# LSH attention and two MLPs: a quarter of the first batch's P transposed by TensorE instead of the DMA, and the low parts of q and V moved to GpSimd there

## The chip, the cores and the metric

One core of one Trainium2 chip runs the whole program. The metric is the device time of one execution in microseconds; lower is better. The kernel before takes 832.61 us, the median of 3 runs (831.09 to 833.43).

## The reference

The inputs are q, k and v of 2 batches, 8 heads, 768 positions and 64 dimensions, a projection of 64 x 6, and the weights of two MLPs (512 to 2048 and back), in float64.

```python
bits   = (q @ proj > 0), (k @ proj > 0)          # 6 bits: a bucket for each position
scores = q @ k.T / sqrt(64), -1e9 where the buckets of q and k differ
attn   = softmax(scores); x = attn @ v           # heads side by side: 1536 x 512
x = gelu_like(x @ w_in) @ w_out                  # h * sigmoid(1.702 h)
x = silu(x @ w_in2) @ w_out2                     # h * sigmoid(h)
```

## The kernel before

Every value is carried as two parts, a rounded high part and a low part that holds the rest, so that several cheap matmuls stand for one exact product. The float64 weights are taken apart on the chip (lines 167 to 178).

The program has three stages. **Stage 0** is attention on the first batch alone, **stage 1** is attention on the second batch with the first MLP on the first batch's tokens running in between (`mlp`, drawn by credits of `RATE`), and **stage 2** is what is left of both MLPs. `stage[0]` turns from 0 to 1 at step 51 of the loop in `attention`, when the 48 steps of the first batch have been written out.

Attention goes in **steps**: step `j` is 128 queries of one head against all 768 keys. There are 96, 48 in each batch; steps 2m and 2m + 1 make a **pair of steps**, 24 in each batch. One step does this:

- `scores` (line 404, 405): TensorE writes the scores, with the mask added by a second matmul, to PSUM.
- `top` (line 422): VectorE takes them from PSUM to `p` and finds the row's extreme.
- `exps` (line 427): ScalarE takes the exponential in place. `p` is 128 x 768 in float32, and there are three buffers of it in stage 0.
- `p_high` (lines 436, 438): `p` is cast to float16, by VectorE for steps with `j % 5` of 2 or 4 (`HIGHV`), else by ScalarE, into the pair's tile `hl` (three buffers in stage 0).
- `p_low` (line 442): GpSimd subtracts the high part from `p`, which gives the low part in float16.
- `p_turn` (line 448): after the second step of a pair, one DMA transposes the whole `hl` tile, 128 x 3072 in float16 (786 KB), into `pt`, of which there are two buffers (`PTB`). SyncE issues it. It comes one step later than the step's other work (`TUL`).
- `av` (lines 460 to 462): TensorE multiplies the 12 blocks of `pt` that belong to the step with V's two parts, 18 matmuls. It is written out three steps after the step's exponential (`LAG`).
- `norm`, `x_turn`, `x_split` (lines 472 to 495): after a head's six steps the rows are scaled, transposed by TensorE into PSUM and split into `XH` (ScalarE) and `XL` (VectorE), as the MLPs read them.

Each head needs preparation, which `ahead` spreads over the 12 steps of the pair of heads before it. `natural` (lines 292, 293) splits q and k into parts: the high part by VectorE, the low part by the engine that `LOWG` names for the stage (GpSimd for k in stage 0 and for k, q in stage 1, if the head is not one of the first two). `turn` (line 300) transposes them on TensorE through a PSUM tile of the pool `ps_m`, which has two buffers, `evict` (line 307) takes them out by ScalarE, `move` copies half of them by ScalarE or a DMA, `bits` and `signs` (lines 332, 339) make the buckets, and `rows` (line 347) moves these by DMA. V is scaled and split by `v_max`, `v_spread`, `v_scale`, `v_high` (line 383, ScalarE) and `v_low`: one VectorE instruction (line 392) in stage 0, a ScalarE scaling in place and a GpSimd subtraction (lines 389, 390) in stage 1.

All transfers but two small ones are issued by SyncE, in one order: the loads of q, k and v, the moves, the rows, the weights and the transposes stand in one queue. Each engine works through its instructions in a fixed order. That order comes from the build: a scheduler arranges the instructions by priority, and `sooner` puts a task of a kind ahead by the number in `SOONER` (for `p_high` 200 in stage 0, `p_low` 75, `p_turn` 35, `natural` 800).

Of the kernel before, what the change touches and what calls it, by code (L numbers as in the profile page):

```python
# [9 lines left out]
F32 = mybir.dt.float32  # L10
F32R = mybir.dt.float32r
F16 = mybir.dt.float16
# [3 lines left out]
ALU = mybir.AluOpType  # L16
# [5 lines left out]
def tile_lsh_attention_two_mlps(  # L22
# [13 lines left out]
    V, A, G, T, SP = nc.vector, nc.scalar, nc.gpsimd, nc.tensor, nc.sync  # L36
# [5 lines left out]
    P = 128  # L42
    NC = S // P
    HS = S // 2
    HC = NC // 2
# [20 lines left out]
    PTB = 2  # L66
    EARLY = 0
    WSTART = 38
    WEVERY = 3
    LOWG = ('k', 'kqv')  # L70
    COPY = ('k', 'q')
    FB = 2
    PB = 2
# [1 line left out]
    GB = 2  # L75

    HIGHV = ((5, (2, 4)), (1, ()))


    SOONER = ({'ahead': 100, 'move': 20, 'load_v': 400, 'evict': 200, 'p_high': 200, 'natural': 800, 'p_turn': 35, 'turn': 100, 'p_low': 75, 'top': 35, 'exps': 75, 'bits': 300, 'norm': 35, 'load': 50, 'signs': 20}, {'scores': 200, 'evict': 50, 'norm': 300, 'av': 400, 'natural': 200, 'gate': 50, 'p_turn': 20, 'load_v': 200, 'load': 20, 'sum': 150, 'move': 20, 'p_high': 150, 'rows': 100, 'p_low': 75, 'bits': 100, 'exps': 20}, {'gate': 300, 'sum': 10, 'weights': 50})  # L80
# [5 lines left out]
    stage = [0]  # L86
# [162 lines left out]
    def attention(sp, s1, ps_m, ps_v, ahead_of, setup):  # L249
        nat, st = {}, {}  # L250
# [12 lines left out]
        N = len(steps)  # L263
# [9 lines left out]
        VS, ident, identr, vtop, pa, pb, thr, thrq, BQ, BK = setup()  # L273
# [13 lines left out]
        def natural(n, nm):  # L287
            x = nat[n, nm]
            hp, lp = (1, 0) if nm == "q" else (0, 1)
            E = G if nm in LOWG[stage[0]] and n > 1 else V  # L290
            t = sp.tile([P, NC, 2, D], F32R, tag="s" + nm, name="s" + nm, bufs=1)
# [93 lines left out]
        def v_low(pr, j):  # L385
            vs, s = st["v", pr]
            x = nat[pr, "v"][:, j]
            if "v" in LOWG[stage[0]]:
                A.activation(x, x, AF.Copy, scale=s[:, j:j + 1])
# [21 lines left out]
        def rotate(tag, bufs, shape, dtype):  # L411
            pool, more = ahead_of["more"].get(tag, (None, 0))
            j = count[tag] = (count.get(tag, -1) + 1) % (bufs + more)
            if j < bufs:
                return sp.tile(shape, dtype, tag=tag, name=tag, bufs=bufs)
            return pool.tile(shape, dtype, tag=tag, name=tag, bufs=more)
# [10 lines left out]
            A.activation(p, p, AF.Exp, bias=lo, scale=-1.0)  # L427


        def p_high(j):  # L430
            if j % 2 == 0:
                st["hl", j] = st["hl", j + 1] = rotate("hl", HLB, [P, 2, 2, 2, HS], F16)
            hl, p = st["hl", j][:, j % 2, 0], st["p", j][0]
            m, own = HIGHV[stage[0]]
            if j % m in own:
                V.tensor_copy(hl, p)
            else:
                A.copy(hl, p)  # L438

        def p_low(j):  # L440
            hl = st["hl", j][:, j % 2]
            G.tensor_tensor(out=hl[:, 1], in0=st.pop(("p", j))[0], in1=hl[:, 0], op=ALU.subtract)  # L442

        def p_turn(j):
            hl = st.pop(("hl", j))
            if j % 2 == 1:
                pt = rotate("pt", PTB, [P, 4 * NC, P], F16)
                latest[0] = SP.dma_start_transpose(out=pt, in_=hl.rearrange("p s a b c -> p (s a b c)")).ins
                st["pt", j - 1], st["pt", j] = pt[:, 0:2 * NC], pt[:, 2 * NC:]
# [109 lines left out]
        for lead, first, last in ((2, 0, N // 2), (1, N // 2, N)):  # L559
            def at(f, j):  # L560
                if first <= j < last:
                    with sooner(f.__name__):
                        f(j)

            for i in range(first - lead, last + LAG + 1):
                if lead == 2:
                    at(scores, i + 2)
                at(av, i - LAG)
                at(top, i + lead - 1)
                m = i - LAG  # L570
                if first <= m < last and m == group[m][-1]:
                    with sooner("norm"):
                        norm(group[m])
                m = i - 2 * (2 - lead)
                if first <= m < last:
                    pr, s = divmod(m, 2 * NC)
                    with sooner("ahead"):
                        if pr + 1 < HEADS // 2:
                            run(ahead(pr + 1, s))
                        if s >= 2 * NC - 4 and pr + 2 < HEADS // 2:  # L580
                            run(ahead(pr + 2, s - 2 * NC))
                at(exps, i)
                at(p_high, i)
                at(p_low, i)
                at(p_turn, i - TUL)
                yield i
                if lead == 1:
                    at(scores, i + 1)
# [107 lines left out]
    with ExitStack() as es:  # L696
        ps_m = es.enter_context(tc.tile_pool(name="ps_m", bufs=2, space=PSUM))
# [8 lines left out]
        for i in attention(sp, s1, ps_m, ps_v, ahead_of, lambda: attention_setup(sp, s1, am, ps_m)):  # L706
            if i == -2:
                for _ in range(EARLY):
                    W.fetch()
            if gen is None and i >= WSTART and i % WEVERY == 0 and W.done < 4:  # L710
                W.step()
            if gen is None and i == SWITCH - 1:
                ps_s.close()
                stage[0] = 1
                ahead_of["lead"] = 1
                ahead_of["more"] = {}
                mb = es.enter_context(tc.tile_pool(name="mlpb", bufs=2))
                ahead_of["pool"] = es.enter_context(tc.tile_pool(name="ps_s1", bufs=1, space=PSUM))
                ps_h = es.enter_context(tc.tile_pool(name="ps_h", bufs=2, space=PSUM))
                gen = mlp(0, [0, 1], [[f, f + 1] for f in range(0, NF, 2)], W, mb, ps_h, True, first1)  # L720
            if gen is not None:
                credit += RATE[i >= 3 * HEADS // 4 * NC]
                while credit >= 1.0:
                    credit -= 1.0
                    next(gen, None)
                    background()
# [41 lines left out]
```

## Time and profile before

| what | us |
|---|---|
| median of 3 runs | 832.61 |
| the profiled execution | 831.93 |
| its span, from the first to the last instruction | 830.1 |

| stage | from, to (us) | length (us) |
|---|---|---|
| 0, attention of the first batch, after the first loads | 20 to 165 | 145 |
| 1, attention of the second batch beside the first MLP | 165 to 415 | 250 |
| 2, the rest of the MLPs | 415 to 830.1 | 415.1 |

The profile is one execution. Busy time of an engine is the union of its instructions' spans; PE is TensorE's matmuls, PEld its weight loads, DVE VectorE, ACT ScalarE, POOL GpSimd, SP SyncE, of which only the queue (SPq) matters here. PEclk is the granted clock of TensorE as a share of full speed. The DMA share is the mean busy share of 16 DMA engines by the time that their packets took. The borders of the stages are read from the work that runs: the first batch's last transpose is issued at 162.6 us, and the last of all at 408.2 us.

### The profile page before, as it was taken

Reading aid. Unit: us, or ns where it says so; the run is one execution under the profiler, and the core shown is the slowest. Engines: PE = TensorE matmul, PEld = TensorE weight load, DVE = VectorE, ACT = ScalarE, POOL = GpSimd, SP = SyncE. Lnnn points to the kernel's source line nnn. Section 1 sums busy time; section 2 is a strip of 40 time slices with the busy share of each in tenths; the row PEclk is TensorE's granted clock in tenths of the full one; section 3 lists DMA queues with packets and bytes.
Section 4 is the critical chain, followed back from the end, with each engine's and each line's share of the span. In section 5 each row is a group of like instructions: output and inputs, shape, how many; then the busy total and the mean of one; then the engine's idle time right before and its main releaser. Section 6 shows DMA issues by size and latency. Waiting matters only on the chain.

```text
span 830.1 us, 13998 instructions
## 1 busy us (share of the span) xinstructions
PE 753.3 (91%) x5384; PEld 692.9 (83%) x5384; DVE 533.9 (64%) x932; ACT 421.4 (51%) x721; POOL 442.0 (53%) x345
## 2 busy tenths in 40 slices
PE   6787787698898998988999999979999999999998
PEld 5677576577797887887999999979999989998996
DVE  8877787988689889779424233899733843422222
ACT  6758656596675666655534232444645433321220
POOL 5656676777777857766733242549534533421120
PEclk9778979599999999999999999999999999999999
DMA  4999999998998979865587421232310400000112
GB/s 117 190 180 193 200 180 223 231 247 238 246 254 231 223 216 226 210 153 109 108 300 261 150 104 49 77 127 95 108 51 21 132 2 1 0 1 1 39 39 76
DMA packets 196270, 116.40 MB, mean 140 GB/s; under 512 B 153318, under 2 KB 175846, under 8 KB 196204
## 3 DMA queue, kind: packets, MB, share of 16 engines
q1 hardware_dynamic: 196044, 115.52, 55.8%
q8 instruction: 42, 0.69, 0.3%
q14 instruction: 24, 0.20, 0.1%
q10 hardware_dynamic: 160, 0.00, 0.0%
HBM read 56.63 MB, written 16.78 MB: 88 GB/s over the span
## 4 chain that ended last, share of the span: by engine, by line
PE 59%; DVE 20%; DMA 10%; ACT 5%; issue 4%; POOL 1%; SPq 1%; DVEq 0%; ACTq 0%; POOLq 0%
PE pso L642 26%; PE psh L608 25%; DMA pt<-hl 6%; DVE f L173 3%; DVE p L422 3%; DVE f L171 3%; DVE f L175 2%; DVE f L172 2%; PE pss L404 2%; PE pss L405 1%; PE psbit L332 1%; POOL hl L442 1%; DMA nk<-in_k_dram 1%; PE pav L460 1%; ACT p L427 1%
## 5 line engine op out<-in xcount | busy, mean ns | idle before, releaser
L619 POOL TENSOR_TENSOR gl<-g,gh 128x384 fp32r<-128x384 f32 x128 | 138.3, 1081 | 201.7 <-ACT gh L618 189.5
L442 POOL TENSOR_TENSOR hl<-p,hl 128x768 f16<-128x768 f32 x96 | 168.0, 1757 | 75.7 <-ACT hl L438 33.2
L608 PE MATMUL psh<-XH,wih 128*128 128x384 f32 x512 | 174.2, 340 | 6.0 <-DVE part L651 3.9
L608 PE MATMUL psh<-XH,wil 128*128 128x384 f32 x512 | 173.0, 338 | 0.0
L608 PE MATMUL psh<-XL,wih 128*128 128x384 f32 x512 | 172.9, 338 | 0.0
L617 DVE TENSOR_TENSOR g<-g,psh 128x384 f32<-128x384 f32 x96 | 52.7, 550 | 116.8 <-ACT g L616 116.7
L651 DVE SCALAR_TENSOR_TENSOR part<-pso,part 128x384 f32<-128x384 f32 (+1 forms) x124 | 72.6, 590 | 83.0 <-PE pso L642 82.8
L427 ACT ACTIVATE p<-p,lo 128x768 f32<-128x768 f32 x96 | 89.7, 937 | 70.4 <-DVE p L422 70.2
L618 ACT CAST gh<-g 128x384 fp32r<-128x384 f32 x128 | 65.5, 512 | 86.7 <-DVE g L617 70.7
L608 PEld LDWEIGHTS psh<-XH,wih 128*128 128x128 f32 x512 | 97.2, 190 | 8.1 <-DVE g L614 2.2
L642 PE MATMUL pso<-gh,woh 128*128 128x384 f32 x256 | 88.6, 352 | 16.9 <-DVE g L614 7.0
L422 DVE TENSOR_SCALAR_CACHE_REDUCE p<-pss 128x768 f32<-128x768 f32 x96 | 90.8, 947 | 14.9 <-PE pss L405 8.6
L608 PEld LDWEIGHTS psh<-XL,wih 128*128 128x128 f32 x512 | 97.2, 190 | 0.6
L608 PEld LDWEIGHTS psh<-XH,wil 128*128 128x128 f32 x512 | 97.2, 190 | 0.0
L616 ACT ACTIVATE g<-psh 128x384 f32<-128x384 f32 x96 | 46.8, 488 | 96.2 <-PE psh L608 95.2
L404 PE MATMUL pss<-ak,aq 128*128 128x384 f32 x192 | 77.4, 404 | 19.7 <-DVE p L422 19.5
L642 PE MATMUL pso<-gl,woh 128*128 128x384 f32 x256 | 86.5, 338 | 0.0
L642 PE MATMUL pso<-gh,wol 128*128 128x384 f32 x256 | 86.5, 338 | 0.0
L460 PE MATMUL pav<-VS,pt 128*128 128x65 f16 x576 | 69.4, 205 | 15.4 <-DMA pt<-hl 13.0
L460 PEld LDWEIGHTS <-pt 128*128 128x128 f16 x576 | 57.4, 105 | 24.1 <-DMA pt<-hl 17.7
L642 PE MATMUL pso<-woh,gh 128*128 128x512 f32 x192 | 74.9, 390 | 0.2 <-ACT gh L618 0.2
L642 PE MATMUL pso<-wol,gh 128*128 128x512 f32 x192 | 75.0, 391 | 0.0
(114 smaller groups left out, 1623.1 us busy)
## 6 DMA issues: line engine op xcount, KB each, us to landing
raw<-in_moe_w_in_dram SPq DMA_DIRECT2D x32, 512.0 KB
raw<-in_moe_w_out_dram SPq DMA_DIRECT2D x32, 512.0 KB
spih<-wih SPq DMA_DIRECT2D x13, 256.0 KB
spil<-wil SPq DMA_DIRECT2D x13, 256.0 KB
spoh<-woh SPq DMA_DIRECT2D x13, 256.0 KB
spol<-wol SPq DMA_DIRECT2D x13, 256.0 KB
wih<-spih SPq DMA_DIRECT2D x13, 256.0 KB
wil<-spil SPq DMA_DIRECT2D x13, 256.0 KB
```

Source lines behind the costliest of these rows:

```text
L404: T.matmul(o, lhsT=lq, rhs=ak[:, half, :], start=True, stop=False)
L422: V.tensor_scalar(p, st.pop(("S", j)), LOW, None, op0=ALU.min, op1=ALU.min, accum_out=lo)
L427: A.activation(p, p, AF.Exp, bias=lo, scale=-1.0)
L442: G.tensor_tensor(out=hl[:, 1], in0=st.pop(("p", j))[0], in1=hl[:, 0], op=ALU.subtract)
L460: T.matmul(o, lhsT=pt[:, i], rhs=hv, start=(i == 0), stop=False)
L608: T.matmul(h, lhsT=a[:, c], rhs=x[t][:, c], start=(n == 0), stop=(n == 3 * NDC - 1))
L616: A.activation(g, h, AF.Sigmoid, scale=beta)
L617: V.tensor_tensor(out=g, in0=g, in1=h, op=ALU.mult)
L618: A.copy(gh[:, f], g)
L619: G.tensor_tensor(out=gl[:, f], in0=g, in1=gh[:, f].bitcast(F32), op=ALU.subtract)
L642: T.matmul(y, lhsT=a, rhs=x, start=(n == 0), stop=(n == 3 * nf - 1))
L651: V.scalar_tensor_tensor(out=acc, in0=y, scalar=scale, in1=acc, op0=ALU.mult, op1=ALU.add)
```

## The change

In stage 0 the pairs of steps 3, 7, 11, 15, 19 and 23 (`TURNT`: of every four pairs the last) are not cast and transposed as before. `p_parts` takes the place of `p_high`, `p_low` and `p_turn` for them. TensorE transposes `p` itself in float32, 128 x 128 at a time, three blocks to a PSUM tile of `ps_m`; ScalarE casts the tile's 128 x 384 to float16 straight into `pt`, and VectorE subtracts that from the PSUM tile and writes the low part into `pt`. A step takes two such tiles. The pair's `pt` buffer is taken when its first step is at `p_high`, not at `p_turn`. Besides, `LOWG` of stage 0 becomes that of stage 1: q's low part (heads after the first two) goes to GpSimd, and V's low part to ScalarE and GpSimd. Nothing in stages 1 and 2 is changed.

```diff
-    LOWG = ('k', 'kqv')
+    LOWG = ('kqv', 'kqv')
+    TURNT = ((4, (3,)), (1, ()))
...
+        def by_tensor(j):
+            m, own = TURNT[stage[0]] if j < N // 2 else TURNT[1]
+            return j // 2 % m in own
+
+        def p_parts(j):
+            if j % 2 == 0:
+                st["whole", j] = st["whole", j + 1] = rotate("pt", PTB, [P, 4 * NC, P], F16)
+            p = st.pop(("p", j))[0]
+            pt = st.pop(("whole", j))[:, j % 2 * 2 * NC:(j % 2 + 1) * 2 * NC]
+            for a in range(2):
+                ps = ps_m.tile([P, 512], F32, tag="m", name="psp")
+                for i in range(HC):
+                    T.transpose(ps[:, i * P:(i + 1) * P], p[:, a, i * P:(i + 1) * P], ident)
+                x = ps[:, 0:HS].rearrange("p (c q) -> p c q", c=HC)
+                hi, lo = (pt[:, n + a * HC:n + (a + 1) * HC] for n in (0, NC))
+                A.copy(hi, x)
+                V.tensor_tensor(out=lo, in0=x, in1=hi, op=ALU.subtract)
+            st["pt", j] = pt
+
         def p_high(j):
+            if by_tensor(j):
+                return p_parts(j)
...
         def p_low(j):
+            if by_tensor(j):
+                return
...
         def p_turn(j):
+            if by_tensor(j):
+                return
```

## Rows read from the trace of the kernel before

**Rows 1.** Busy time of each engine in stretches of the run (us from the span's start): the stretch, its length, busy us and number of instructions of PE, PEld, DVE, ACT and POOL, the granted clock of TensorE, the DMA share and the GB/s moved.

```profile
20.00:165.00 145.00, 111.35 (x1186) 96.76 (x1187) 118.86 (x216) 96.33 (x140) 96.17 (x61) 0.80 1.00 198
50.00:140.00 90.00, 71.90 (x841) 60.86 (x840) 72.60 (x140) 63.76 (x93) 60.52 (x38) 0.89 1.01 192
165.00:415.00 250.00, 222.90 (x1980) 204.38 (x1979) 203.80 (x358) 164.23 (x271) 174.43 (x125) 0.97 0.86 205
415.00:830.10 415.10, 406.00 (x2147) 381.52 (x2145) 193.88 (x301) 148.71 (x291) 160.69 (x142) 1.00 0.24 82
```

**Rows 2.** The same view for two shorter stretches: 400 to 412 us, where a transpose is nearly the only transfer, and 435 to 445 us, where there are loads and no transpose.

```profile
400.00:412.00 12.00, 12.00 (x118) 11.84 (x115) 5.63 (x13) 6.56 (x10) 8.59 (x7) 1.00 0.60 113
...
435.00:445.00 10.00, 10.00 (x60) 10.00 (x59) 5.65 (x9) 5.76 (x13) 3.07 (x3) 1.00 1.05 378
```

**Rows 3.** The transposes of stage 0 as SyncE issues them: all of them from 20 to 165 us, and those from 50 to 140 us, with their number, their shortest, median and longest time in the queue in ns and the start of the first and the last; then the queue in order of time, the first transpose, a stretch from 79.52 us and the last transpose of the batch.

```profile
L448 SPq DMA_TRANSPOSE pt<-hl x24: 3580/4182/4584, 21.6 to 162.6; - x24
L448 SPq DMA_TRANSPOSE pt<-hl x16: 3580/4105/4532, 50.8 to 133.0; - x16
...
21.57 4.58 SPq L448 DMA_TRANSPOSE pt<-hl  x1
...
79.52 3.92 SPq L448 DMA_TRANSPOSE pt<-hl  x1
83.97 0.33 SPq L268 DMA_DIRECT2D nq<-in_q_dram  x1
84.49 4.43 SPq L448 DMA_TRANSPOSE pt<-hl  x1
...
162.59 3.90 SPq L448 DMA_TRANSPOSE pt<-hl  x1
```

**Rows 4.** The longest pieces of the chain that ended last between 40 and 165 us: start, us, what.

```profile
34.85 7.83 DMA pt<-hl
83.97 3.59 DMA nq<-in_q_dram
98.46 3.78 DMA nk<-in_k_dram
104.38 2.92 DMA nv<-in_v_dram
109.00 6.35 DMA pt<-hl
123.97 6.38 DMA pt<-hl
137.00 4.54 DMA nv<-in_v_dram
```

**Rows 5.** Who waited for whom from 20 to 165 us: us in total, times, the longest.

```profile
ACT p L427 <- DVE p L422: 27.7, 17, 4.7
...
DVE am L364 <- DMA nv<-in_v_dram: 9.8, 4, 4.2
PE pav L460 <- DMA pt<-hl: 9.6, 6, 3.6
...
DVE sk L292 <- DMA nk<-in_k_dram: 3.9, 3, 2.4
...
DVE sq L292 <- DMA nq<-in_q_dram: 2.4, 3, 1.1
```

**Rows 6.** Groups of instructions from 0 to 165 us: line, engine, operation, out<-in, number | busy us, mean ns of one | idle us before them and what ended it.

```profile
L442 POOL TENSOR_TENSOR hl<-p,hl 128x768 f16<-128x768 f32 x50 | 86.0, 1729 | 43.3 <-DVE hl L436 24.5 <-ACT hl L438 14.7 <-issue 4.1
L427 ACT ACTIVATE p<-p,lo 128x768 f32<-128x768 f32 x50 | 46.6, 935 | 27.7 <-DVE p L422 27.7
L438 ACT CAST hl<-p 128x768 f16<-128x768 f32 x31 | 25.6, 827 | 1.0 <-DMA pt<-hl 0.5
L436 DVE CAST hl<-p 128x768 f16<-128x768 f32 x19 | 12.9, 679 | 2.1 <-ACT p L427 1.1 <-ACT BK L314 1.0
L392 DVE SCALAR_TENSOR_TENSOR VS<-nv,sv,VS 128x384 f16<-128x384 f32 x10 | 12.4, 1243 | 0.0
L293 POOL TENSOR_TENSOR sk<-nk,sk 128x384 fp32r<-128x384 f32 x10 | 10.3, 1028 | 14.2 <-DVE sk L292 6.1 <-PE pstr L371 5.7 <-PE pstr L300 1.6
L293 DVE TENSOR_TENSOR sq<-nq,sq 128x384 fp32r<-128x384 f32 x11 | 9.9, 901 | 0.1
```

**Rows 7.** Instructions of stage 0 that work as the new ones will: the transposes of `x_turn` from float32, and the two that take their parts out of PSUM; number, shortest, median and longest in ns, first and last start. Then one head's six transposes and one `v_low` of VectorE in the order of time (start, us).

```profile
L488 PE MATMUL psx<-ident,xn x21: 272/273/476, 65.5 to 160.2; 128*128 128x128 f32 x21
L494 ACT CAST XH<-psx x7: 469/479/495, 67.8 to 160.6; 128x384 fp32r<-128x384 f32 x7
L495 DVE TENSOR_TENSOR XL<-psx,XH x7: 540/544/547, 69.1 to 161.8; 128x384 fp32r<-128x384 f32 x7
...
65.47 0.87 PE L488 MATMUL psx<-ident,xn 128*128 128x128 f32 x6
...
66.21 0.61 DVE L392 SCALAR_TENSOR_TENSOR VS<-nv,sv,VS 128x384 f16<-128x384 f32 x1
```

**Rows 8.** V's low part as stage 1 makes it, from 165 to 420 us (columns as in rows 6), and q's low part on VectorE between 4 and 14 us, before GpSimd has its first `p_low`.

```profile
L390 POOL TENSOR_TENSOR VS<-nv,VS 128x384 f16<-128x384 f32 x6 | 6.8, 1151 | 2.4 <-ACT nv L389 2.4
L389 ACT ACTIVATE nv<-nv,sv 128x384 f32<-128x384 f32 x6 | 3.6, 620 | 0.0
...
L293 DVE TENSOR_TENSOR sq<-nq,sq 128x384 fp32r<-128x384 f32 x2 | 1.1, 558 | 0.0
```

## The prediction

> **What bounds the kernel now.** I read the stretches first, stage by stage [rows 1]. In stage 2 TensorE is busy 406.0 of 415.1 us at full clock; the change does not touch it. In stage 1 TensorE is busy 222.9 of 250 us and VectorE 203.8. Stage 0, where the change lies, is another case: no engine is above VectorE's 118.9 of 145 us (82%), TensorE has 111.4 at a granted clock of 0.80, ScalarE and GpSimd 96 each, but the DMA share is 1.00 while only 198 GB/s are moved. With loads alone the same engines move 378 GB/s at a share of 1.05 [rows 2]. So in stage 0 the DMA engines are occupied by something slow, and that is the transposes.
>
> Next the queue [rows 3]: the 24 transposes of the batch are issued from 21.57 to 162.59 us, one every 141.0 / 23 = 6.13 us, and each holds SyncE's queue for 4.18 us (median). The loads stand behind them: nq at 83.97 us goes out when the transpose begun at 79.52 is through. The chain of waits names the same thing [rows 4]: its seven longest pieces are transfers, three of them transposes of 6.35 to 7.83 us, the others loads. By the waits [rows 5] TensorE stood 9.6 us for transposed P and VectorE 9.8 + 3.9 + 2.4 = 16.1 us for loads of v, k and q. I take stage 0 as held back first by transposes and what is queued behind them, and second, not far off, by VectorE.
>
> **The transposes removed.** Six pairs of 24 no longer use the DMA. What one costs the DMA engines, from below: in the stretch of 400 to 412 us a share of 0.60 moves 113 GB/s [rows 2], so 786 KB take 0.786 x 0.60 / 0.113 = 4.2 us. From above: 50 to 140 us moved 192 GB/s x 90 us = 17.3 MB [rows 1], its 16 transposes [rows 3] 12.6 MB of it; the other 4.7 MB at 378 / 1.05 = 360 GB/s take 13 us, which leaves (91 - 13) / 16 = 4.9 us. Six of them: 25 to 29 us of transfers, and 6 x 4.18 = 25 us of SyncE's queue. That is the most that the stage can win from this. It is not all to be had, because other limits come up first.
>
> The Trainium skill ("Advanced Engine Details and Errata", X-Bar Transpose (TRN2)) says that a transposing DMA is as fast as a regular one, at 350 to 400 GB/s; a transpose would then take 2.0 to 2.2 us, an estimate from that page, and the six some 13 us. The trace disagrees: 188 GB/s at full share by rows 2.
>
> **VectorE in stage 0.** Removed: ten V low parts, 12.4 us; nine of the eleven q low parts (the first two heads stay) at 901 ns, 8.1 us; five of the 19 casts (among the 12 turned steps, those with j % 5 of 2 or 4 are 7, 14, 22, 39 and 47) at 679 ns, 3.4 us [rows 6]. Added: 24 subtractions from PSUM. The nearest row is XL, 544 ns, also from PSUM and 128 x 384 [rows 7]; 13.1 us. The output is narrower, so it may be a little less; a wait for GpSimd could make it 1.0 us each at most, as L293 shows. Sum: -10.8 us; between -13 and 0 with these ends.
>
> **ScalarE.** Removed: seven casts at 827 ns, -5.8 us [rows 6]. Added: 24 casts from PSUM at 479 ns (XH), 11.5 us [rows 7]; ten scalings of V at 620 ns [rows 8], 6.2 us. Sum +11.9 us on 96.3, so 108: now level with VectorE, but in no place the only one.
>
> **GpSimd.** Removed: 12 low parts at 1729 ns, -20.7 us. Added: nine of q at 1028 ns (k's row), 9.3 us [rows 6], and ten of V at 1151 ns, 11.5 us [rows 8]. Sum near 0. At the start V's first two low parts leave VectorE, which has then more room; the chain may gain 1 to 2 us there, which I leave out.
>
> **TensorE.** Added: 72 transposes from float32. Six follow each other in 0.87 us, so (0.87 - 0.27) / 5 = 0.12 us each [rows 7], 8.6 us in all, twice that at half clock. TensorE stands still for 33 us of stage 0 [rows 1], so I cost this at nothing; if the cover goes, 9 to 17 us. The pool ps_m, with its two buffers, gets 24 more tiles, each held for about 0.4 + 0.48 + 0.54 = 1.4 us; `turn` and `bits` queue for the same two.
>
> **Sum.** The stage can't go faster than its busiest engine allows. VectorE's work becomes 118.9 - 10.8 = 108.1 us. In stage 1 VectorE holds a share of 203.8 / 250 = 0.815 with the DMA share lower (0.86), and in stage 0 now 0.82; I take it that this web of short instructions does not pack VectorE closer. 108.1 / 0.815 = 132.6 us in place of 145: **-12.4 us**. This is less than half of what the DMA is freed by, and about what the waits for transfers in rows 5 (9.6 + 16.1 = 25.7 us, not all on the path) allow. What is late next is the handing over from `top` to `exps`: ScalarE already waits 27.7 us for VectorE there [rows 5]. Stages 1 and 2 do the same work from the same step on, so the gain reaches the end. The profiled execution has 831.93 us, of which 1.8 lie outside its span, and is 0.7 under the median; against the median, 832.6 - 12.4 = **820.2 us**. A measurement can tell about 0.3% (2.5 us) from no change.
>
> **Rivals.**
>
> (a) The whole relief of the DMA comes through, -25 to -29 us: 804 to 808 us. For it: the chain's longest pieces are all transfers [rows 4]. Against: VectorE would have to be busy 108 of 118 us (92%) and ScalarE as much.
>
> (b) Nothing is won. VectorE and GpSimd slow each other: q's low part takes 558 ns on VectorE before GpSimd has its long instructions [rows 8] and 901 in the stage as a whole [rows 6]; V's takes 0.61 us in one instance [rows 7] and 1243 ns on average. If such waiting does not go away with the moved work but falls on VectorE's other instructions, the move relieves VectorE only by its own work, 9 x 0.56 + 10 x 0.61 = 11.1 instead of 20.5 us, and VectorE's sum is -1.4: (118.9 - 1.4) / 0.815 = 144.2, -0.8 us, 831.8 us. The Trainium skill ("Perfetto Trace Analysis", Optimizing Scalar/DVE Operations) warns that moving work between these two engines might not help because they share a read port; by that rule this would be the outcome. Against it: GpSimd's total stays as it is, so the same occupied time meets 24 fewer VectorE instructions of that kind.
>
> (c) Slower, by one mechanism: ScalarE stands at the first cast of a turned pair m. That cast writes `pt`, whose buffer pair m - 2 holds until its transpose has landed (6.35 us after issue, rows 4) and `av` has read it. Behind the cast on ScalarE stand the next exponentials and casts; GpSimd's low parts and the transpose of pair m + 1 wait for those. From the release to that transpose ScalarE needs four casts from PSUM (1.9 us), three exponentials (2.8) and two casts (1.65), then GpSimd one low part (1.7): 8.1 us. Pair m - 1's transpose covers 4.2 us of it if it is issued in time. The DMA stands empty for the rest. One turn saves at most 4.9 us of DMA, so from 4.9 us of emptiness a turn loses; with m - 1's transpose half over, 8.1 - 2.1 = 6.0, it loses 1.1 us, six times 7 us: 839 us; with no cover (8.1 - 4.9) x 6 = 19 us: 852 us. Against it: the loads that are now late would fill that gap, and the turned pair itself needs no landing, so its `av` can follow at once.
>
> That the change does not do what it says can hardly be: the turned steps are fixed by their numbers.
>
> **How the numbers follow.** The forecast has 0.58, with a range of its own of 815 to 828 us (VectorE at a share of 0.85 with its sum at -10.8, or at 0.80 with -7). Rival (a) has 0.12, (b) 0.13, (c) 0.17. The range of 8 in 10 is 808 to 834 us: it leaves out most of (a) and most of (c). Faster by over 0.3%: 0.58 + 0.12 + 0.05 of (b), 0.75. Within 0.3%: the rest of (b), 0.08. Slower: 0.17.
>
> **What would show it.** Right: 18 transposes instead of 24 in the first batch, and the last one issued (now that of pair 22) so early that stage 1 begins near 152 us; the DMA share of stage 0 down to 0.9 or less; VectorE's waits for nv, nk and nq cut to half; the stretch of stage 2 still 415 us long. The new VectorE subtraction near 0.54 us, the new ScalarE cast near 0.48. Rival (a): stage 0 under 122 us with VectorE above 90%. Rival (b): VectorE's casts and copies from SBUF grow in mean, and stage 0 stays at 145. Rival (c): ScalarE's longest wait before the new cast, put down to `pav` or to transposed P, 4 us or more, six times. The forecast is wrong altogether if stage 1 or 2 changes its length by more than 3 us, since their work is the same.

## The result, and the profile after

The changed kernel takes 840.87 us (median of 4, 839.77 to 841.39) against 832.55 (4 runs): ratio 1.010, 95% interval 1.0082 to 1.0118, **8.3 us slower**. Forecast were 820.2 us and a range of 808 to 834. Its profiled execution has 840.68 us and a span of 838.9, 8.8 more than before.

The lines of the new code are 444 (TensorE's transpose of P), 447 (ScalarE's cast) and 448 (VectorE's subtraction); `top` is now line 424, the DMA transpose 476, `av` 488 to 490. The first question is where the 8.8 us arise. A mark that both traces show is the first `top` of the second batch, step 48. VectorE in order of time, before and then after (start, us):

```profile
147.47 0.94 DVE L422 TENSOR_SCALAR_CACHE_REDUCE p<-pss 128x768 f32<-128x768 f32 x1
...
153.80 0.94 DVE L422 TENSOR_SCALAR_CACHE_REDUCE p<-pss 128x768 f32<-128x768 f32 x1
```

```profile
156.15 0.94 DVE L424 TENSOR_SCALAR_CACHE_REDUCE p<-pss 128x768 f32<-128x768 f32 x1
...
159.85 0.92 DVE L424 TENSOR_SCALAR_CACHE_REDUCE p<-pss 128x768 f32<-128x768 f32 x1
```

Step 48 comes 6.0 us later, and from there to the end it takes 838.9 - 159.85 = 679.1 us in place of 830.1 - 153.8 = 676.3, 2.8 more. So by this mark there are two losses, and most is in the first batch, which was to become 12 us shorter. The split hangs on the mark, because step 48 begins while TensorE still has `av` of the first batch to do. The last of those (the 864th `pav` matmul: 48 steps of 18) ends at 173.0 us before and 175.0 after, only 2.0 us later:

```profile
172.82 0.19 PE L462 MATMUL pav<-VS,pt 128*128 128x65 f16 x1
```

```profile
174.84 0.19 PE L490 MATMUL pav<-VS,pt 128*128 128x65 f16 x1
```

The engines up to step 48, before and then after (columns as in rows 1):

```profile
20.00:153.80 133.80, 103.75 (x1132) 89.73 (x1132) 108.49 (x202) 91.23 (x133) 86.44 (x55) 0.82 1.00 194
```

```profile
20.00:159.80 139.80, 104.98 (x1189) 91.24 (x1189) 97.81 (x204) 98.49 (x157) 86.25 (x64) 0.89 0.77 160
```

VectorE has 10.7 us less to do, GpSimd the same, ScalarE 7.3 us more (a share of 0.70 after 0.68), and the DMA share fell from 1.00 to 0.77. No engine is busy for much more than three quarters of the stretch, yet it is longer: the engines wait more. For whom, the chain of work that ended last says. From 40 to 155 us, by line, as shares of that stretch, before and then after (the view ends its line there):

```profile
by line: DMA pt<-hl 17.9%; POOL hl L442 8.5%; issue 8.3%; DMA nv<-in_v_dram 6.5%; DVE p L422 6.2%; DMA nk<-in_k_dram 5.8%; SPq L448 4.5%; PE psbit L332 4.5%; PE pss L404 4.2%; PE pav L460 3.4%; DVE hl L436 3.4%; DVE f L171 3.2%; DMA nq<-in_
```

```profile
by line: DMA pt<-hl 37.7%; issue 6.8%; DMA nv<-in_v_dram 5.5%; PE psbit L334 5.0%; PE pav L488 4.6%; DVE p L424 4.2%; PE pav L489 3.5%; PE pav L490 3.5%; PE pss L406 3.0%; SPq L349 2.5%; DVE f L175 2.4%; PE pss L407 2.3%; DVE f L173 1.9%; S
```

With a quarter of the transposes gone, the remaining ones have more than twice the share of the chain (37.7% after 17.9%). Other work no longer covers them: around the turned pairs they follow one another with a wait between. Around the turned pair 7 (steps 14, 15) the queue and TensorE run as follows (order of time; in brackets the idle time before and what ended it):

```profile
55.13 5.36 SPq L476 DMA_TRANSPOSE pt<-hl  x1
...
62.71 0.24 PE L488 MATMUL pav<-VS,pt 128*128 128x65 f16 x1 [3.30 <-DMA pt<-hl]
...
64.62 0.25 PE L490 MATMUL pav<-VS,pt 128*128 128x65 f16 x1
...
64.94 3.66 SPq L476 DMA_TRANSPOSE pt<-hl  x1
...
75.95 3.69 SPq L476 DMA_TRANSPOSE pt<-hl  x1
```

Pair 5's transpose goes out at 55.13 us and has landed at 62.7, when TensorE has waited 3.3 us for it; its `av` runs to 64.87. Only then, at 64.94, does **pair 6's** transpose go out, and pair 8's at 75.95. In the kernel before, these come about every 6 us [rows 3]. The code says why. `p_parts(14)` takes the `pt` buffer for pair 7 at step 14, but `p_turn(13)`, which takes pair 6's, is written after it in the same turn of the loop (`TUL`). So of two buffers, pair 7 takes the one that pair 4 leaves, and pair 6 has to wait until `av` has read pair 5; pair 8 then waits for pair 7's. Around such a pair the transposes run one at a time, and TensorE waits until each has landed. SyncE's waits for `av` from 20 to 165 us show it (total, times, longest), before and then after:

```profile
SPq L448 <- PE pav L462: 0.6, 2, 0.3
```

```profile
SPq L476 <- PE pav L490: 8.7, 5, 2.2
```

### The profile page after: what moved, and what is told of

It is laid out like the page before. It is cut to its first block, busy times and chain, and to the rows that moved or that the text cites. A ratio compares the mean times of both kernels' runs of the same rounds, so it can differ in the third digit from the quotient of the medians.

```text
span 838.9 us, 14174 instructions
## 1 busy us (share of the span) xinstructions
PE 753.1 (90%) x5456; PEld 691.8 (82%) x5456; DVE 528.6 (63%) x932; ACT 432.7 (52%) x748; POOL 437.6 (52%) x352
## 4 chain that ended last, share of the span: by engine, by line
PE 56%; DVE 19%; DMA 11%; issue 6%; ACT 5%; POOL 2%; SPq 1%; POOLq 0%; DVEq 0%; ACTq 0%
PE pso L670 25%; PE psh L636 25%; DMA pt<-hl 9%; DVE p L424 4%; DVE f L175 4%; DVE f L177 2%; DVE f L173 2%; DVE f L174 2%; DVE part L679 1%; DVE g L642 1%; PE psbit L334 1%; DMA nk<-in_k_dram 1%; PE pav L488 1%; PE pss L406 1%; ACT p L429 1%
## 5 line engine op out<-in xcount | busy, mean ns | idle before, releaser
L468 POOL TENSOR_TENSOR hl<-p,hl 128x768 f16<-128x768 f32 x84 | 144.0, 1719 | 84.1 <-ACT hl L462 31.5
L670 PE MATMUL pso<-gh,woh 128*128 128x384 f32 x256 | 89.9, 357 | 13.1 <-DVE g L642 4.8
L406 PE MATMUL pss<-ak,aq 128*128 128x384 f32 x192 | 74.7, 390 | 27.6 <-DVE p L424 27.2
L488 PE MATMUL pav<-VS,pt 128*128 128x65 f16 x576 | 65.9, 200 | 24.6 <-DMA pt<-hl 24.5
L488 PEld LDWEIGHTS <-pt 128*128 128x128 f16 x576 | 55.0, 101 | 34.2 <-DMA pt<-hl 29.4
```

The lines of the kernel that those rows point to most:

```text
L406: T.matmul(o, lhsT=lq, rhs=ak[:, half, :], start=True, stop=False)
L488: T.matmul(o, lhsT=pt[:, i], rhs=hv, start=(i == 0), stop=False)
L670: T.matmul(y, lhsT=a, rhs=x, start=(n == 0), stop=(n == 3 * nf - 1))
```

## The experiments

Theories on record: **B** (the `pt` buffers), **Q** (P's transposes stand in TensorE's queue behind `av`), **L** (the low parts on GpSimd), and for the time after step 48 **O** (the order that the scheduler happens to give) against **S** (a cost handed over from the first batch).

One table for all, from the profiles: step 48, what follows it, the span; from the timed runs, median and ratio to the kernel before, as timed beside them, with its interval. A profile is one run of 4 to 10, not always a typical one: e11's is the slowest of its six (841.17 us, median 837.56), e6's the fastest of its four (836.04, median 838.87).

```
                       step 48   after it   span    median   ratio to before
before                  153.8     676.3    830.1
the change              159.8     679.1    838.9    840.87   1.0100 [1.0082, 1.0118]
e1_order                162.7     674.5    837.2    840.09   1.0100 [1.0066, 1.0134]
e2_pt3                  148.2     679.5    827.7    829.66   0.9969 [0.9941, 0.9996]
e3_lowg_only            157.3     679.0    836.3    838.15   1.0074 [1.0046, 1.0101]
e4_turn_only            156.6     678.7    835.3    837.90   1.0078 [1.0051, 1.0104]
e5_before_pturn22       153.2     677.2    830.4    833.10   1.0009 [0.9996, 1.0022]
e6_before_av401         153.4     680.8    834.2    838.87   1.0084 [1.0062, 1.0105]
e7_pt3_scores205        151.6     676.8    828.4    831.83   1.0003 [0.9981, 1.0024]
e8_before_pt3           151.7     675.2    826.9    831.99   1.0000 [0.9985, 1.0016]
e9_turn_own             154.3     684.7    839.0    842.60   1.0127 [1.0084, 1.0170]
e10_both_own            149.0     680.4    829.4    830.97   0.9973 [0.9950, 0.9996]
e11_after_scores230     158.1     681.3    839.4    837.56   1.0054 [1.0012, 1.0095]
e12_turn_own_scores230  155.8     677.6    833.4    836.32   1.0046 [1.0027, 1.0065]
e13_lowg_pt3            154.9     672.7    827.6    831.98   1.0007 [0.9978, 1.0035]
e14_both_own_scores230  152.1     675.1    827.2    830.46   0.9976 [0.9949, 1.0004]
e15_pt3_av404           150.4     674.2    824.6    826.36   0.9924 [0.9895, 0.9953]
e16_pt3_rate342         150.2     675.1    825.3    827.71   0.9945 [0.9925, 0.9965]
```

**e1: the claims in order.**

```diff
+                at(p_turn, i - TUL)
                 at(p_high, i)
                 at(p_low, i)
-                at(p_turn, i - TUL)
```

> The change with one thing different: p_turn of the step before is written out ahead of p_high, so the pair before a turned pair takes its pt buffer first. Theory B (buffers): in the change the turned pair m takes the pt buffer before pair m-1 does, so the transpose of m-1 has to wait until av has read pair m-2, and that of m+1 until av has read m; the transposes then run one by one with an av between them. With the order mended SyncE no longer waits for pav before a transpose, the first batch ends 8 to 15 us sooner than in the change, 825 to 833 us in all. Rival Q (TensorE's queue): what costs is that P's transposes stand on TensorE behind an av that waits for the DMA, so ScalarE and VectorE stand; the order of the buffers changes little, 838 to 843 us.

840.09 us, step 48 even later. As I had put B, it failed: the order alone is not it. SyncE's waits for `pav` did not go, and a new one came up on ScalarE (20 to 165 us):

```profile
SPq L476 <- PE pav L490: 13.3, 6, 5.3
...
ACT pt L447 <- PE pav L490: 8.1, 4, 5.2
```

Now the turned pair m takes the buffer of pair m - 2, and ScalarE's cast stands until that is read: this is the wait of the prediction's rival (c), four times, not six, and with the waits on SyncE beside it. By the code, with two buffers one of the two has to wait, whichever claims first.

**e2: a third buffer.** `'pt': 0` becomes `'pt': 1` in `MORE`, which adds a buffer in the first stage alone.

> The change with a third pt buffer in the first stage. Theory B: with three buffers the early claim takes none that the pair before needs; 822 to 832 us, SyncE's waits for pav gone. Rival Q: av still waits for the landing and P's transposes stand behind it, 837 to 842 us.

829.66 us, 11 us under the change, step 48 at 148.2 us. Its step 48 on VectorE, its chain from 40 to 148 us, and SyncE's waits for `pav` from 20 to 155 us:

```profile
148.17 0.92 DVE L424 TENSOR_SCALAR_CACHE_REDUCE p<-pss 128x768 f32<-128x768 f32 x1
```

```profile
by line: DMA pt<-hl 17.0%; issue 9.1%; DMA nv<-in_v_dram 7.5%; PE psbit L334 5.5%; PE pss L406 5.1%; DVE p L424 4.4%; PE pss L407 4.4%; PE pav L488 4.3%; DVE sk L294 4.0%; PE pav L490 3.6%; PE pav L489 3.6%; SPq L349 3.4%; PE pstr L302 3.1%
```

```profile
SPq L476 <- PE pav L490: 3.5, 1, 3.5
```

The transposes' share of the chain is back at 17%. B in its wider form (two buffers don't suffice for a pair that its engines fill themselves, block by block) holds. Q falls as the cause here: P's transposes stand on the same TensorE, with the same `av` written ahead of them. Q's own sign, ScalarE waiting for P's transposes, is 6.3 us in the change and 3.5 in e2.

**e3 and e4: the two parts alone.** e3 is the kernel before with `LOWG = ('kqv', 'kqv')`, e4 the change with `LOWG = ('k', 'kqv')`.

> The kernel before with q's and V's low parts on GpSimd in the first stage and no turned pair. If the loss lies in this part (rival L): 836 to 842 us. By theories B and Q it has no share in it: VectorE has 20 us less of work, GpSimd 21 us more, 828 to 834 us.

> The turned pairs alone, q's and V's low parts as in the kernel before. Theories B and Q: the whole loss is here, 839 to 846 us. Rival L (the low parts on GpSimd cost): 828 to 834 us.

Both lose 6 us, so no theory had it right. At step 48 they are 3.5 and 2.8 us late; the sum is near the change's 6.0, but single profiles scatter by as much as each of these (below). In e3 the DMA share stays high although VectorE is relieved; what costs it 6 us stays open. In e4 VectorE stays as busy as before (107.0 of 135 us) and the transposes wait for `pav` 13.1 us. The stretch from 20 to 155 us, e3 and then e4:

```profile
20.00:155.00 135.00, 99.37 (x1131) 83.68 (x1130) 91.43 (x187) 94.89 (x144) 102.94 (x74) 0.87 0.97 194
```

```profile
20.00:155.00 135.00, 102.56 (x1185) 88.76 (x1186) 107.01 (x220) 92.84 (x144) 66.27 (x44) 0.91 0.80 159
```

**e8 and e13: controls.** The kernel before with the third buffer, and that with the low parts on GpSimd, neither with a turned pair.

> Control for e2_pt3: the kernel before with a third pt buffer in the first stage and no turned pair. If the third buffer alone is what made e2_pt3's first stage short, the first MLP matmul comes near 147 us here too; by theory B (the change needs a third buffer, the kernel before does not) it comes at 153 to 157 us, since the transposes here follow each other in order and the DMA is busy all the time.

> Low parts of q and V on GpSimd in the first stage and a third pt buffer, no turned pair. If the turned pairs are what shortens the first batch (theory B), the DMA stays at a share near 1 and the first batch's last av ends at 168 to 173 us (157.1 in e2_pt3, 170.3 in e8_before_pt3). If the low parts with the buffer do it, 157 to 162 us.

Step 48 comes at 151.7 and 154.9 us: the buffer alone brings about 2 us there and nothing in the time (831.99 us), and the low parts on top of it nothing (831.98). Against e3 the buffer does help e13, by 6 us, most of it after step 48 (672.7 us, e3 679.0); why is not shown. In e13 the first batch's last `av` ends at 168.8 us (157.1 in e2) with the DMA still full from 20 to 155 us, as B says. The turned pairs are needed for e2's 148.2.

```profile
20.00:155.00 135.00, 99.50 (x1167) 83.45 (x1168) 94.76 (x189) 95.51 (x143) 106.45 (x75) 0.91 1.01 202
```

**e9 and e10: a `pt` buffer of their own for the turned pairs**, the others rotating through two as before; e9 without, e10 with the low parts on GpSimd.

```diff
-                st["whole", j] = st["whole", j + 1] = rotate("pt", PTB, [P, 4 * NC, P], F16)
+                st["whole", j] = st["whole", j + 1] = ahead_of["more"]["p"][0].tile(
+                    [P, 4 * NC, P], F16, tag="own", name="own", bufs=1)
```

> The turned pairs alone (low parts of q and V as in the kernel before), with a pt buffer of their own; the other pairs rotate through two as before. Theory B: the turned pairs cost because they take a buffer of the rotation early; with their own, and against e4_turn_only whose step 48 has its scores taken at 156.6 us, that comes at 143 to 149 us; SyncE's waits for pav before a transpose under 3 us in all (13.1 in e4). In all 824 to 832 us, the rest after step 48 being 675 to 681 us by the scheduler's order. Rival Q (TensorE's queue): 154 to 157 us for step 48, 835 us or more.

> The whole change with a pt buffer of its own for the turned pairs. Theory B: step 48 at 145 to 150 us (159.8 in the change). Against e9 it tells what q's and V's low parts on GpSimd cost or bring once the buffers are out of the way: by e3 (3.5 us later at step 48) they cost 1 to 4 us; by the forecast's sum for VectorE they bring 3 us or more.

e10 does as B says (149.0). e9 misses: its waits for `pav` are gone (1.4 us in all), yet step 48 is at 154.3 and the whole takes 842.60, both where Q had been put. The stretch of 20 to 155 us, e9 and then e10, and ScalarE's wait for P's transposes in it, in the same order:

```profile
20.00:155.00 135.00, 103.82 (x1189) 89.87 (x1189) 110.23 (x223) 93.80 (x146) 70.64 (x45) 0.89 0.83 168
```

```profile
20.00:155.00 135.00, 107.23 (x1268) 93.20 (x1268) 102.66 (x215) 103.45 (x167) 88.97 (x65) 0.91 0.85 180
```

```profile
ACT own L447 <- PE psp L444: 11.4, 10, 3.9
```

```profile
ACT own L447 <- PE psp L444: 2.9, 8, 0.6
```

In e9 VectorE is at 110.2 of 135 us, 0.817: the share that the forecast took as its ceiling. Moving the low parts then brings 154.3 - 149.0 = 5.3 us at step 48 (155.8 - 152.1 = 3.7 in e12 and e14, the same two with another order later) and takes most of ScalarE's wait away, with P's transposes in the same places. That VectorE and not TensorE's queue held e9 follows from this pair of runs alone. So the parts of the change need each other, and both need the buffer.

**e5, e6, e11: another order of the same work.** One priority of the second stage changed by a little (`p_turn` 20 to 22, `av` 400 to 401; in the change `scores` 200 to 230). The first stage's instructions and their order stay: the traces of e5, e6 and e11 first differ in order from those of their kernels at about 175 us or later.

> The kernel before with one priority of the second stage set from 20 to 22 (p_turn). The work and the first stage's order are the same; the scheduler's order differs from about a third of the second stage on. Theory O (order): the second stage's length hangs on the order that the scheduler happens to give, and the kernel before has a short one (258.5 us from the first MLP matmul to the last av, against 265 to 269 in four of the five variants so far): 834 to 840 us, that stage 262 to 269 us. Rival S: the second stage became longer in the change by a cause in its first stage (buffers, queues or engines handed over late); then this kernel is as the one before, 831 to 834 us.

> The kernel before with another priority of the second stage set from 400 to 401 (av): again the same work and the same first stage, another order from midway in the second stage on. Theory O: another length of the second stage, somewhere between 258 and 269 us, 831 to 840 us. Rival S: 831 to 834 us.

> The change as it is, with one priority of the second stage set from 200 to 230 (scores): the same work, the same first stage, another order in the second. Theory O: step 48 at 160 us again, the rest after it at another length within 674 to 681 us (679.1 in the change), 836 to 843 us. Rival S: 679 us again, 840 to 841 us.

e5 misses O's range and lies in S's: 833.10 us. The time after step 48 is 677.2 and 680.8 us where the kernel before has 676.3, and e6 is 6.8 us slower as a whole (838.87 against 832.09, no run of the one among those of the other) without one instruction more on any engine that computes; its step 48:

```profile
153.44 0.94 DVE L422 TENSOR_SCALAR_CACHE_REDUCE p<-pss 128x768 f32<-128x768 f32 x1
```

e11 has 681.3 against 679.1 in its slowest run, but its median is 3.3 us below the change's. So O rests on e6: order alone can cost nearly as much as the change's whole loss, and need not.

**e7, e12, e14, e15, e16: the same on e2, e9 and e10**, to see whether an early end of the first batch costs later (S).

> The change with a third pt buffer (e2_pt3) and one priority of the second stage set from 200 to 205 (scores): the first stage as in e2_pt3, another order of the second. Theory O: the first MLP matmul at 147 us as in e2_pt3, the second stage at another length than 266.0 us; with a short one (259) 822 us, with a long one 830. Rival S: the second stage again 266 us, 829 to 830 us.

> e9 with the same priority set from 200 to 230: a second draw of the second stage's order on the same first stage. Theory O: step 48 as in e9, the rest another length within 674 to 681 us; so 822 to 832 us. The better of e9 and e12 may beat the kernel before by 3 to 8 us.

> e10_both_own with one priority of the second stage from 200 to 230: the first batch as in e10 (step 48 at 149 us, last av 158). Theory O: the time after step 48 is another draw between 674 and 685 us, so 823 to 834 us. Rival S (an early end of the first batch costs in the second stage): 679 us or more again, 829 to 834 us.

> e2_pt3 with the priority of av in the second stage from 400 to 404, the order the same until late in that stage. First batch as in e2. Theory O: after step 48 between 674 and 685 us; 823 to 834 us. Rival S: 679 us or more.

> e2_pt3 with 3.42 instead of 3.4 MLP pieces per step in the first part of the second stage: another order from its start on. First batch as in e2. Theory O: after step 48 between 674 and 685 us; 823 to 834 us. Rival S: 679 us or more.

After step 48: 676.8, 677.6, 675.1, 674.2 and 675.1 us. e12 misses its range as a whole (836.32 us). The six kernels with the early first batch (e2, e7, e10, e14 to e16) have 676.9 on average, the four with the batch of before (before, e5, e6, e8) 677.4. By this mark S falls. By the first batch's last `av` it would not: the six end it 12 us earlier on average (159.7 us, the four 171.9), and their spans are 3.3 us shorter. What speaks against S all the same is e2 and e15: in the traces their order is the same up to 337 us, and with nearly as early a first batch (last `av` at 160.6 and 157.1 us) e15 is faster. e15 has the best of both: 826.36 us, ratio 0.9924, **faster than the kernel before and the changed one**; e16 is next. But e15 is the best of these six; their ratios have a mean of 0.9965, some 3 us. The step 48 of e15, from which 824.6 - 150.4 = 674.2 us remain:

```profile
150.44 0.92 DVE L424 TENSOR_SCALAR_CACHE_REDUCE p<-pss 128x768 f32<-128x768 f32 x1
```

With the first stage's order unchanged, step 48 of e2 and its three variants still lies between 148.2 and 151.6 us, so a difference of 3 us between single profiles is not to be read as an effect.

## Why the prediction was wrong

- **The prices were right.** The new subtraction takes 551 ns (544 forecast), the new cast 478 (479), the transposes 273, as `x_turn`'s [rows 7]:

```profile
L444 PE MATMUL psp<-ident,p x72: 270/273/448, 36.2 to 162.2; 128*128 128x128 f32 x72
...
L447 ACT CAST pt<-psp x24: 453/478/485, 37.6 to 162.7; 128x384 f16<-128x384 f32 x24
...
L448 DVE TENSOR_TENSOR pt<-psp,pt x24: 515/551/558, 39.2 to 164.4; 128x384 f16<-128x384 f32 x24
```

  VectorE's sum up to step 48 is -10.7 us (-10.8 forecast), GpSimd's -0.2 (0), ScalarE's +7.3 (+11.9).
- **The step that failed is the "Sum".** It turned VectorE's relief into time by a share of 0.815, on the belief that the DMA, once freed of six transposes, would leave VectorE as the next limit. VectorE's share fell to 97.8 / 139.8 = 0.70. What was late next was not an engine but a buffer: `pt` has two, and a turned pair holds one from its first step on. I had counted the transposes' time on the DMA and in SyncE's queue, and not how long each buffer is held. e2 and e10 show the size: with the buffer step 48 comes 5.6 and 4.8 us before that of the kernel before, in place of 6.0 after it, and the whole takes 829.66 and 830.97 us in place of 840.87. The -12.4 us do not come even so: over the six kernels with the early first batch it is 2.8 us on average at step 48 (150.2 us, the four with the batch of before 153.0), and some 3 us in the end.
- **Rival (c) had the right resource in the wrong place.** It put the wait on ScalarE's first cast. There the trace has 1.1 us, once; the wait stands on SyncE, before the transpose of pair m - 1, since the turned pair claims first. e1 produced (c)'s wait (8.1 us on ScalarE in four, the longest 5.2) beside 13.3 us on SyncE, and costs as much as the change. That (c) gave 839 us and the change took 840.9 is in part chance: some 3 us are of another origin.
- **"Stages 1 and 2 do the same work, so the gain reaches the end" failed too.** The same work came in another order. At an unchanged first stage e6 has 4.5 us more after step 48 from order alone; the 2.8 us here lie within that, and within the scatter of single profiles. That they are order and nothing else is not shown; there was no kernel with the change's first stage and the old second one. By the first batch's last `av` 6.8 of the 8.8 us come behind it, and the forecast's own sign of being wrong altogether (a change of stage 1 by more than 3 us) came: all of attention ends at 426.0 us in place of 415.1, which is 4.9 us more even from step 48 on.
- **Rival (b)** is not what happened. From 0 to 165 us VectorE's cast of k grew from 742 to 869 ns on average, but that of q fell from 758 to 535 and that of P from 679 to 642, and VectorE's total fell as forecast. The Trainium skill ("Perfetto Trace Analysis", Optimizing Scalar/DVE Operations) warned that moving work between VectorE and GpSimd might not help. The runs split: at step 48 it brought 5.3 us with VectorE at a share of 0.82 (e9 to e10) and nothing with the DMA at a share of 0.99 (e8 to e13).
- Of the signs, the DMA share of 0.9 or less came (0.77) without the gain that it was to show. The last transpose was issued at 164.6 us, 2 us later than before and not early enough for stage 1 to begin near 152. VectorE's waits for nv, nk and nq fell only from 16.1 [rows 5] to about 13 us.
- The 0.3% that the forecast called measurable is too fine for single runs: the kernel before alone ran from 826.97 to 835.96 us in one comparison. The ratios' intervals are 0.1 to 0.4% wide on either side.

## What to carry to other kernels

When one item of a pipeline is taken off its slow resource, ask how long it holds each shared buffer and in which order the claims are written, not only what the resource is freed of; a falling share of the DMA with a growing share of its transfers in the chain is the sign that items no longer overlap. Where a scheduler orders the instructions, compare a change with a few orders of the same work, since its side effects elsewhere can be as large as its effect. Two edits that fail one by one can win a little together when each meets a different limit (here the buffer, VectorE and the DMA).

## What the runs showed that was not expected

- A DMA transpose of 786 KB holds SyncE's queue not much shorter where the DMA share is 0.77 than where it is 1.00: median 3.7 us against 4.18 [rows 3], below. That time says little of how busy the DMA is.
- TensorE's granted clock up to step 48 rose from 0.82 to 0.89, while the stretch became longer; the clock was not what held it.

```profile
L476 SPq DMA_TRANSPOSE pt<-hl x18: 3579/3706/5361, 20.7 to 164.6; - x18
```

- Part of the time after step 48 hangs on the clock. Near the end of attention in e2, TensorE works only 0.81 us between 409 and 412 us and waits 2.2 us for a transpose of P; from 412 to 422 us it is granted 0.50, the lower of its two levels (1.2 of 2.4 GHz). In e15 it is busy throughout the same 3 us and keeps full clock. The stretches 409 to 412 and 412 to 422 us, e2 with its wait and then e15:

```profile
409.00:412.00 3.00, 0.81 (x15) 0.49 (x14) 0.56 (x1) 1.02 (x2) 2.87 (x4) 0.99 0.77 143
412.00:422.00 10.00, 7.83 (x49) 7.30 (x47) 1.31 (x4) 1.62 (x2) 0.00 (x0) 0.50 0.54 176
...
411.61 0.20 PE L488 MATMUL pav<-VS,pt 128*128 128x65 f16 x1 [2.19 <-DMA pt<-hl]
```

```profile
409.00:412.00 3.00, 3.00 (x47) 3.00 (x48) 1.31 (x4) 0.20 (x2) 1.22 (x2) 1.00 0.00 0
412.00:422.00 10.00, 9.26 (x55) 8.93 (x54) 3.33 (x6) 5.15 (x10) 5.04 (x5) 1.00 0.78 272
```

  e6 has the same beside the kernel before: TensorE waits 3.6 us for its last transposes, and 412 to 422 us have 0.78 in place of 1.00. The runs of one kernel differ in this too: e2's ten go from 826.68 us (mean granted clock 0.975) to 833.37 (0.965). So what follows step 48 in a single profile is not the order's alone.
